# Duo attention and routed experts on one core: v loaded in 512-byte runs and ordered by TensorE, streaming heads scored in blocks of 64 queries

## The chip, the core and the metric

The kernel runs on one core of a Trainium2 chip. The metric is the device time in microseconds (us) of one execution; lower is better. Its engines run in parallel, each through its own instruction stream in order: PE (TensorE, matmuls and transposes into PSUM), DVE (VectorE), ACT (ScalarE), POOL (GpSimd) and SP (SyncE, which here only issues DMAs). They meet through semaphores. PSUM has eight banks of 2 KB a partition, and every buffer in it belongs to a pool with a fixed number of banks.

## What is computed

The reference is an attention with two kinds of heads, followed by a mixture of experts:

```python
# q, k, v: (4, 8, 768, 64); is_retrieval = [1, 0, 1, 0, 0, 0, 1, 0]; n_sink 4; window 64
causal = rel >= 0                       # rel = query position - key position
stream_keep = causal & (is_sink | (rel < window))
mask = causal for a retrieval head, stream_keep for a streaming head
a = softmax(where(mask, q @ k.T / 8, -1e9)); attn = a @ v
x = attn.transpose(0, 2, 1, 3).reshape(3072, 512)
do_compute = x @ w_skip > 0             # the other rows are handed through
e_idx = argmax(x @ w_gate); gate_w = softmax(x @ w_gate)[e_idx]
out = x + gate_w * (relu(x @ w1[e_idx]) @ w2[e_idx])   # for rows that compute
```

So a query of a retrieval head sees all earlier keys, and a query of a streaming head sees the last 64 keys and keys 0 to 3, the sinks. There are 12 retrieval and 20 streaming heads.

## The kernel before

**Pairs and steps.** The 32 heads are taken as 16 pairs of neighbouring heads (`heads`, L474). In each batch three pairs hold a retrieval and a streaming head, and one (pairs 2, 6, 10 and 15) holds two streaming heads. The loop at L852 runs 18 steps. Step i scores pair i, weighs pair i-1, transposes q and k of pair i+1 and casts those of pair i+2. Two steps behind come the transposes of the result for the gate.

**The order is written by hand.** The block at L832 puts PE, DVE, POOL and ACT under `manual_schedule`: on these four an instruction stands where the program writes it. SP isn't among them. The order in a step: `step(0)` (the first score chunk), k transposes, `step(1)`, q transposes, `weigh(i-1, 0)`, `step(2)`, `cast_qk(i+2)`, `step(3)`, `gate_transpose(i-2)`, `weigh(i-1, 1)`, `step(4)`. Every fourth step adds the choice of an expert for a batch (`choose`, L717), the step after it the places of the tokens (`gate_weight`, `place`, `left`, `right`; L754 to L828). `left` makes six compares on DVE that write Lall (L812), `right` makes oht (L818) and Rall (L822).

**q and k.** SP loads fp32 tiles (L484), POOL casts them to fp16 (L499), PE transposes them into a `tr_ps` bank, named tps (L518). ACT copies q from there (L526). DVE copies k (L535) into `kz`, one half of the partitions for each head and zeros in the other; in a pair of two streaming heads ACT copies the second half (L537).

**v.** SP loads v with the position within a block of 128 as the partition (L395, L492), in runs of 64 fp32, 256 bytes. At the start of step i POOL casts it into `va` (L505), which also holds a column of ones for the sum of the weights. For a streaming head POOL copies `va` to `vx` (L510) and overwrites its first four partitions with the sinks' values (L511).

**Scores.** A chunk is up to 1024 columns of a `st_ps` buffer, pst, of which there are two, each two banks. PE first writes a mask (L578, the identity times a mask of 0 and -30000), and adds k times q to it (L588). ACT takes the exponential into `at` (L606). A retrieval head has 2688 columns, three chunks. A streaming head has 1408, two chunks of 1024 and 384: six diagonal blocks of 128 x 128, and five blocks that hold the previous block's last 64 keys on 64 partitions (L595) and, on the other 64, the sinks (L600).

**Weighing.** `weigh` (L609) multiplies `at` with `va` or `vx`, 65 columns a matmul (L626), into one of two `ov_ps` banks, opsa: 21 matmuls for a retrieval head, 11 for a streaming head. DVE takes the reciprocal of the sums (L637, rec) and scales (L641, xh). POOL casts the scaled pair to fp16 (L649, gx) for the gate, and SP stores xh (L654, L660). Behind five of these casts POOL issues a load of expert weights (L650). PE transposes gx into a `tr_ps` bank (L667, xtp) and ACT copies it out (L675).

**The experts.** After the last batch's places, POOL gathers the chosen rows (L958), PE runs two matmuls an expert (L994, L1014), ACT applies relu (L1001), DVE adds (L1022), POOL scatters (L1024), and between them POOL loads the remaining weights.

**PSUM in the attention.** st_ps takes four banks, tr_ps two, ov_ps two. In tr_ps stand all of tps, xtp, the gate's logits gps and the counts kps, in turn.

Of the kernel before, what the change touches and what calls it, by code (L numbers as in the profile page):

```python
# [259 lines left out]
def kernel(  # L260
# [100 lines left out]
    for e in range(E // 2):  # L361
        for half in range(2):
            wtile(e, half, wpool)
    wtile(E // 2, 0, wpool)
# [30 lines left out]
    vv = v.rearrange("b h (n p) d -> b p h n d", p=P)  # L395
# [11 lines left out]
    SLEN = (2 * NQB - 1) * P  # L407
    CH = 1024

    with tc.tile_pool(name="ac", bufs=1) as ac_pool, \  # L410
# [5 lines left out]
         tc.tile_pool(name="tr_ps", bufs=2, space=bass.MemoryType.PSUM) as tr_psum, \  # L416
         tc.tile_pool(name="at", bufs=2) as at_pool, \
         tc.tile_pool(name="ov_ps", bufs=2, space=bass.MemoryType.PSUM) as ov_psum, \
# [20 lines left out]

        NPR = B * H // 2  # L440
        qk32, v32, qk16, qT, ats, xhs, x16s, xTs = ({} for _ in range(8))
        gpss = {}

        def make_masks():
# [5 lines left out]
            def select(m, base, column, row):  # L450
                nc.gpsimd.affine_select(
                    out=m, in_=m, compare_op=ALU.is_ge, fill=-MASKED,
                    base=base, pattern=[[column, P]], channel_multiplier=row)
# [4 lines left out]
            band = ac_pool.tile([P, P], FP16, name="band")  # L458
            nc.gpsimd.memset(band, 0.0)
            select(band, 0, 1, -1)  # L460
            select(band, WINDOW - 1, -1, 1)
            saux = ac_pool.tile([P, P], FP16, name="saux")
            nc.gpsimd.memset(saux, 0.0)
            select(saux, WINDOW - 1 - P, -1, 1)
            nc.gpsimd.memset(saux[:N_SINK], 0.0)
            smask = ac_pool.tile([P, 2 * NQB - 1, P], FP16, name="smask")
            nc.vector.tensor_copy(
                smask[:, :NQB], band.unsqueeze(1).to_broadcast([P, NQB, P]))
            nc.vector.tensor_copy(smask[:N_SINK, 0], rmask[:N_SINK])
            nc.vector.tensor_copy(  # L470
                smask[:, NQB:], saux.unsqueeze(1).to_broadcast([P, NQB - 1, P]))
            return smask.rearrange("p n c -> p (n c)"), rmask
# [15 lines left out]
        def load_v(i):  # L488
            b, hs = heads(i)
            vf = ld_pool.tile([P, 2, NQB, D], FP32, tag="vf", name="vf")  # L490
# [12 lines left out]
        def cast_v(i):  # L503
            va, vx = vab[i % 2], vxb[i % 2]
            nc.gpsimd.tensor_copy(va[:, :, :, :D], v32[i])  # L505
            if i % 4 == 3:
                nc.scalar.activation(xgs[(i + 1) // 4], xgs[0], ACT.Copy)
            for hi, hh in enumerate(heads(i)[1]):
# [598 lines left out]
```

## Time and profile before

| | |
|---|---|
| median of three runs | 208.47 us (208.34 to 209.57) |
| the profiled execution | 209.57 us |
| its span, first to last instruction | 208.0 us |
| busy: PE, DVE, ACT, POOL | 169.1, 113.1, 113.7, 120.0 us |
| mean granted clock of PE | 0.928 |
| first exponential (ACT L606) | 9.09 us |
| last value before the gather (DVE flagi) | 131.0 us |
| last matmul of the experts | about 198 us |
| q, k loads; v loads | 16 each of 384 KB; 32 of 192 KB |
| DMA packets under 512 bytes | 28,500 of 48,000 |

The page of a profile gives busy times, the span in 40 slices (each digit a busy share in tenths, PEclk the clock granted to PE), and groups of instructions. A line of the waits reads: engine and line that waited, who ended the wait, us in total, how often, the longest. A line of the timeline reads: start, duration, engine, line, operation, what it writes and reads, how many were merged, and in brackets the idle time before it with its releaser. A line of the windows reads: stretch, its length, busy time and number of instructions of each engine, PEclk, DMA share, GB/s. In all of them L-numbers are lines of the kernel.

### The profile page before, as it was taken

How to read it: one execution, taken by the hardware profiler on the slowest of the kernel's cores; microseconds unless marked ns; L12 is line 12 of the kernel's file. 1: busy time of each engine (PE TensorE's matmuls, PEld its weight loads, DVE VectorE, ACT ScalarE, POOL GpSimd, SP SyncE). 2: the span in 40 equal slices, each digit the busy share in tenths (PEclk: the TensorE clock that was granted, in tenths of full speed). 3: DMA queues.
4: the chain of work that ended last, by engine and by line, in shares of the span. 5: the costliest groups of instructions: out<-in, count | busy, mean ns of one | idle time of the engine just before them, and what ended most of it. 6: DMA issues, size and time to landing. Idle time of an engine off the chain costs nothing.

```text
span 208.0 us, 4783 instructions
## 1 busy us (share of the span) xinstructions
PE 169.1 (81%) x1904; PEld 121.7 (59%) x1904; DVE 113.1 (54%) x278; ACT 113.7 (55%) x164; POOL 120.0 (58%) x180
## 2 busy tenths in 40 slices
PE   6596979978991878996989737988999999999920
PEld 2365657756671656674776524367587688675700
DVE  5333756635899435899835878233555344544020
ACT  2358769995993395996699528214242243140400
POOL 7584698759565439564573502588868675133311
PEclk9969999999997599999699985699999999999995
DMA  5999599999899996899869989999999999999601
GB/s 180 293 340 294 136 178 285 318 337 313 227 237 262 292 276 172 257 268 189 241 119 215 223 189 190 196 212 217 267 242 231 230 234 238 227 250 251 169 8 61
DMA packets 48000, 47.12 MB, mean 227 GB/s; under 512 B 28500, under 2 KB 43604, under 8 KB 47074
## 3 DMA queue, kind: packets, MB, share of 16 engines
q0 software_dynamic: 7120, 21.56, 49.3%
q1 hardware_dynamic: 40850, 25.17, 43.5%
q8 instruction: 17, 0.28, 0.5%
q14 instruction: 13, 0.11, 0.2%
HBM read 56.64 MB, written 10.49 MB: 323 GB/s over the span
## 4 chain that ended last, share of the span: by engine, by line
DMA 17%; DVE 12%; issue 9%; POOL 8%; PE 6%; ACT 1%; POOLq 1%; DVEq 0%
DMA out_dram<-xg,idx_s 14%; POOL xg L958 4%; DMA xg<-out_dram,idx_s 4%; POOL out_dram L1024 3%; DVE Lall L812 3%; DVE xh L641 2%; PE opsa L626 1%; DVE kz L535 1%; PE pst L588 1%; DVE oht L818 1%; PE tps L518 1%; PE pst L578 1%; DVE Rall L822 1%; POOLq L1067 1%; DVE val L762 1%
## 5 line engine op out<-in xcount | busy, mean ns | idle before, releaser
L606 ACT ACTIVATE at<-pst 128x1024 f16<-128x1024 f32 (+2 forms) x76 | 61.9, 836 | 17.9 <-PE pst L588 10.7
L1001 ACT ACTIVATE ht<-hps 128x512 f16<-128x512 f32 x32 | 19.1, 598 | 45.4 <-PE hps L994 45.4
L588 PE MATMUL pst<-qT,kz 128*128 128x128 f16 (+2 forms) x288 | 36.3, 243 | 3.3 <-DVE kz L535 2.8
L535 DVE COPY kz<-tps 64x768 f16<-64x768 f16 x28 | 26.7, 953 | 18.6 <-PE tps L518 18.3
L588 PEld LDWEIGHTS <-kz 128*128 128x128 f16 x288 | 24.1, 101 | 17.7 <-issue 7.0
L649 POOL CAST gx<-xh 128x768 f16<-128x768 f32 x15 | 12.4, 826 | 35.5 <-DVE xh L641 30.7
L994 PE MATMUL hps<-xT,w 128*128 128x256 f16 x256 | 29.3, 273 | 1.1 <-DVE xT L984 1.1
L994 PEld LDWEIGHTS <-w 128*128 128x128 f16 x256 | 27.9, 113 | 2.7 <-issue 1.4
L1014 PE MATMUL yps<-w,ht 128*128 128x512 f16 x128 | 28.8, 379 | 0.0
L1024 POOL DMA_INDIRECT out_dram<-xg,idx_s x16 | 16.5, 1031 | 19.1 <-issue 9.1
L578 PE MATMUL pst<-smask,ident 128*128 128x512 f16 (+1 forms) x60 | 22.1, 368 | 4.3 <-ACT at L606 4.2
L1022 DVE SCALAR_TENSOR_TENSOR xg<-yps,gsl,xg 128x512 f32<-128x512 f32 x16 | 12.0, 751 | 20.5 <-PE yps L1014 20.4
L958 POOL DMA_INDIRECT xg<-out_dram,idx_s x16 | 17.1, 1071 | 9.0 <-DVE flagi L933 4.5
L1014 PEld LDWEIGHTS <-ht 128*128 128x128 f16 x128 | 12.3, 98 | 13.5
L626 PE MATMUL opsa<-va,at 128*128 128x65 f16 x372 | 20.0, 197 | 0.0
L641 DVE TENSOR_TENSOR xh<-opsa,rec 128x384 f32<-128x384 f32 x32 | 17.8, 557 | 1.3
L626 PEld LDWEIGHTS <-at 128*128 128x128 f16 x472 | 18.4, 100 | 0.2
L637 DVE RECIPROCAL rec<-opsa 128x6 f32<-128x6 f32 x32 | 6.2, 195 | 20.1 <-PE opsa L626 19.8
L526 ACT ACTIVATE qT<-tps 128x768 f16<-128x768 f16 x16 | 13.0, 814 | 5.8 <-PE tps L518 5.8
L675 ACT ACTIVATE gxT<-xtp 128x768 f16<-128x768 f16 x15 | 12.1, 809 | 6.2 <-PE xtp L667 6.2
L974 DVE CAST x<-xg 128x512 f16<-128x512 f32 x16 | 9.7, 639 | 10.5 <-DMA xg<-out_dram,idx_s 10.5
L667 PE MATMUL xtp<-ident,gx 128*128 128x128 f16 x96 | 8.5, 227 | 8.4 <-DVE kz L535 4.8
(121 smaller groups left out, 278.8 us busy)
## 6 DMA issues: line engine op xcount, KB each, us to landing
w<-in_moe_w_dram POOLq DMA_DIRECT2D x13, 1024.0 KB, 10.8
qf<-in_q_dram SPq DMA_DIRECT2D x16, 384.0 KB, 5.7
kf<-in_k_dram SPq DMA_DIRECT2D x16, 384.0 KB, 5.9
vf<-in_v_dram SPq DMA_DIRECT2D x32, 192.0 KB, 5.5
out_dram<-xh SPq DMA_DIRECT2D x7, 768.0 KB, 4.9
w<-in_moe_w_dram POOLq DMA_DIRECT2D x6, 512.0 KB, 9.0
out_dram<-xh SPq DMA_DIRECT2D x2, 384.0 KB, 5.4
xg<-out_dram,idx_s POOLq DMA_INDIRECT x16, 7.6
```

What stands on the lines that cost most here:

```text
L526: nc.scalar.activation(t16.rearrange("d (p n) -> d p n", n=NQB), ti, ACT.Copy)
L535: nc.vector.tensor_copy(to, ti[r])
L578: nc.tensor.matmul(pst[:, bank - c0:bank - c0 + mw], C.ident, rmask.unsqueeze(1).to_broadcast([P, mw // P, P]) if retr else smask[:, bank: ...
L588: nc.tensor.matmul(pst[:, cols], kz[:, j * P:(j + 1) * P], qT[i][:, qb * P:(qb + n) * P], start=mw <= 0, stop=mw <= 0 or last)
L606: nc.scalar.activation(ats[i][:, b0:b0 + cn], pst[:, :cn], ACT.Exp, scale=SCALE)
L626: nc.tensor.matmul(opsa[:, qb, :], ats[i][:, b0 + c:b0 + c + P], vb, start=(n == 0), stop=(n == len(plan) - 1))
L641: nc.vector.tensor_mul(xhs[i // 2][:, :, 2 * (i % 2) + hi, :], opsa[:, :, :D], rec.to_broadcast([P, NQB, D]))
L958: ins = nc.gpsimd.indirect_dma_start(out=xgs[t], out_offset=None, in_=out[:, :], in_offset=bass.IndirectOffsetOnAxis(ap=idx_s[:, t:t + 1], ...
L994: nc.tensor.matmul(hps[:, fi, :], wts[e, 0][:, s].rearrange("p (t c r) -> p t r c", c=P, r=WR)[:, fs // WR, fs % WR], xTs[e][:, s, :], sta ...
L1001: nc.scalar.activation(ht[:, 2 * f2:2 * f2 + 2], hps, ACT.Relu)
L1014: nc.tensor.matmul(ypss[s2], hts[e][:, fs, s2 * P:(s2 + 1) * P], wts[e, 1][:, fs, :], start=(fs == 0), stop=(fs == FS - 1))
L1024: ins = nc.gpsimd.indirect_dma_start(out=out[:, :], out_offset=bass.IndirectOffsetOnAxis(ap=idx_s[:, t:t + 1], axis=0), in_=xgs[t], in_off ...
```

## The change

**v.** The load now puts two neighbouring positions in one run of 512 bytes: partition p of a block of 256 positions holds positions 2p and 2p+1. POOL casts the tile as it stands into `vin` (`cast_v`), now for pair i+1 in step i, behind `cast_qk(i+2)`. In step i, behind the k transposes, `order_v(i)` brings the positions in order: two matmuls with 0/1 matrices (`pick`) for each half of the blocks of 128, 384 columns each, into two `tr_ps` banks. ACT copies the first half into `va`, DVE the second. Then POOL makes `vx` (`shift_v`), which holds the block of 128 positions shifted by 64, in two copies on 64 partitions. The zeroing copy of xg on ACT keeps its place at the start of a step (`zero`).

**Streaming heads.** Scores are made in blocks of 64 queries against 128 keys, which cover the window, and the sinks' scores of five blocks of 128 queries are packed in two further blocks, on 4 partitions from each of 0, 32, 64 and 96. That makes 1024 columns, one chunk. The sinks' values lie in a new tile `vsk` for all heads, zero elsewhere, zeroed by DVE and filled by four DMAs from POOL at the start. The masks are made anew for it. A streaming head is weighed by 16 matmuls.

**Pools.** tr_ps has three banks and ov_ps one; the last head's sums go to a st_ps buffer. Two tiles of expert weights (w2 of expert 3, w1 of expert 4) go from the first weight pool to the one that opens when the attention's pools are closed; the order of the loads stays.

The core of the diff (left out: the score loop's parts for streaming heads that go, and names):

```diff
-    vv = v.rearrange("b h (n p) d -> b p h n d", p=P)
+    vv = v.rearrange("b h (m p n) d -> b p h m (n d)", p=P, n=2)
...
-    SLEN = (2 * NQB - 1) * P
+    SLEN = (NQB + 2) * P
...
-         tc.tile_pool(name="tr_ps", bufs=2, space=bass.MemoryType.PSUM) as tr_psum, \
+         tc.tile_pool(name="tr_ps", bufs=3, space=bass.MemoryType.PSUM) as tr_psum, \
...
-         tc.tile_pool(name="ov_ps", bufs=2, space=bass.MemoryType.PSUM) as ov_psum, \
+         tc.tile_pool(name="ov_ps", bufs=1, space=bass.MemoryType.PSUM) as ov_psum, \
...
+        def clear_sinks():
+            for hs in (slice(1, H, 2), slice(4, 5)):
+                nc.vector.memset(vsf[:, :, hs].bitcast(FP32), 0.0)
+            for g in range(4):
+                nc.vector.memset(
+                    vsk[32 * g:32 * g + N_SINK, :, :, g, D:], 1.0)
+
+        def sink_values():
+            for g in range(4):
+                nc.gpsimd.dma_start(
+                    out=vsk[32 * g:32 * g + N_SINK, :, :, g, :D].rearrange(
+                        "p b h d -> p (b h) d"),
+                    in_=v.rearrange("b h s d -> s (b h) d")[:N_SINK])
...
         def cast_v(i):
+            v16[i] = qk_in_pool.tile([P, 2, NQB // 2, 2, D], FP16, tag="vin",
+                                     name="vin")
+            nc.gpsimd.tensor_copy(
+                v16[i].rearrange("p h m n d -> p h m (n d)"), v32[i])
+
+        def order_v(i):
+
             va, vx = vab[i % 2], vxb[i % 2]
-            nc.gpsimd.tensor_copy(va[:, :, :, :D], v32[i])
+            for half in range(2):
+                vps = tr_psum.tile([P, 2, NQB // 2, D], FP32, tag="tps",
+                                   name="vps")
+                for n in range(2):
+                    nc.tensor.matmul(vps, pick[:, half, n],
+                                     v16[i][:, :, :, n], start=n == 0,
+                                     stop=n == 1)
+                to = va[:, :, half::2, :D]
+                if half == 0:
+                    nc.scalar.activation(to, vps, ACT.Copy)
+                else:
+                    nc.vector.tensor_copy(to, vps)
+            shift_v(i)
...
+        def shift_v(i):
+            va, vx = vab[i % 2], vxb[i % 2]
             for hi, hh in enumerate(heads(i)[1]):
                 if not IS_RETR[hh]:
-                    nc.gpsimd.tensor_copy(vx[:, hi], va[:, hi, :NQB - 1])
-                    nc.gpsimd.tensor_copy(
-                        vx[:N_SINK, hi], va[:N_SINK, hi, 0:1].to_broadcast(
-                            [N_SINK, NQB - 1, D + 1]))
+                    nc.gpsimd.tensor_copy(vx[:D, hi], va[:D, hi, 1:])
+                    nc.gpsimd.tensor_copy(vx[D:, hi], va[D:, hi, :NQB - 1])
...
+        def score_near(i, hi, pst):
+
+            kz, qt = kzb[i % 2][:, hi], qT[i]
+            for bank in range(2):
+                nc.tensor.matmul(
+                    pst[:, bank * 512:(bank + 1) * 512], C.ident,
+                    smask[:, bank * 512:(bank + 1) * 512], start=True,
+                    stop=False)
+            nc.tensor.matmul(pst[:, :P], kz[:, :P], qt[:, :P], start=False,
+                             stop=False)
+            for t in range(3, 2 * NQB, 2):
+                cols = slice(t * D, (t + 1) * D)
+                nc.tensor.matmul(pst[:, cols], kz[:, (t - 1) * D:(t + 1) * D],
+                                 qt[:, cols], start=False, stop=False)
+            for t in range(2, 2 * NQB, 2):
+                cols = slice(t * D, (t + 1) * D)
+                for r, u in ((0, t), (D, t - 1)):
+                    nc.tensor.matmul(pst[r:r + D, cols],
+                                     kz[:, u * D:(u + 1) * D], qt[:, cols],
+                                     start=False, stop=t == 6)
+            for qb in (5, 1, 2, 3, 4):
+                g, c = (qb - 1) % 4, NQB + (qb - 1) // 4
+                nc.tensor.matmul(
+                    pst[32 * g:32 * g + 32, c * P:(c + 1) * P], kz[:, :32],
+                    qt[:, qb * P:(qb + 1) * P], start=False, stop=qb < NQB - 1)
...
+                vs = vsk[:, b, hs[hi]]
+                plan = [(qb, (NQB + (qb - 1) // 4) * P, vs[:, (qb - 1) % 4])
+                        for qb in range(1, NQB)]
+                plan.append((0, 0, va[:, hi, 0]))
+            near = [] if IS_RETR[hs[hi]] else [
+                (t, vx[:, hi, t // 2 - 1] if t % 2 == 0 else va[:, hi, t // 2])
+                for t in range(2, 2 * NQB)]
+            if i == NPR - 1 and hi == 1:
+                last_ps = st_psum.tile([P, CH], FP32, tag="pst", name="opsl")
...
+            for t, vb in near:
+                r = (t % 2) * D
+                nc.tensor.matmul(
+                    opsa[r:r + D, t // 2, :],
+                    ats[i][:, b0 + t * D:b0 + (t + 1) * D], vb, start=False,
+                    stop=t >= 2 * NQB - 2)
...
             lower_mask()
+            clear_sinks()
             load_qk(2)
             transpose(0, "q")
             transpose(0, "k")
+            cast_v(0)
+            load_v(2)
             cast_qk(1)
+            sink_values()
             for i in range(NPR + 2):
                 cur = chunks(i) if i < NPR else []
-                if i < NPR:
-                    cast_v(i)
                 if i + 3 < NPR:
                     load_qk(i + 3)
-                if i + 2 < NPR:
-                    load_v(i + 2)
+                if i < NPR:
+                    zero(i)
...
                 step(0)
                 if i + 1 < NPR:
                     transpose(i + 1, "k")
+                if i < NPR:
+                    order_v(i)
...
                 if i + 2 < NPR:
                     cast_qk(i + 2)
+                if i + 1 < NPR:
+                    cast_v(i + 1)
+                if i + 3 < NPR:
+                    load_v(i + 3)
...
-        for e in range(E // 2, E):
+        for e in range(E // 2 - 1, E):
```

## The prediction

> **What bounds the kernel now.** I read the page first, then the waits, then the timeline engine by engine, and last a table of windows around the stalls. In the page's slices (1 slice = 5.2 us) the experts fill slices 26 to 38 and the attention all before them:
>
> ```profile
> PE   6596979978991878996989737988999999999920
> DVE  5333756635899435899835878233555344544020
> ACT  2358769995993395996699528214242243140400
> POOL 7584698759565439564573502588868675133311
> PEclk9969999999997599999699985699999999999995
> ```
>
> From 138 us on PE is full at full clock (58.87 us busy of 60.00 in the window 138 to 198). The change touches nothing there, so the end moves by what the attention moves. In the attention no engine is the bound alone. A step with a retrieval and a streaming head (step 4, 34.52 to 39.87 us) keeps PE going without a wait for 5.35 us, and ACT needs about 5.1. Where a step takes longer, these waits say why:
>
> ```profile
> POOL gx L649 <- DVE xh L641: 30.7, 13, 5.3
> PE xtp L667 <- DVE kz L535: 4.8, 1, 4.8
> PE pst L578 <- ACT at L606: 4.7, 7, 1.2
> POOL qin L499 <- DMA qf<-in_q_dram: 2.2, 3, 1.4
> POOL kin L499 <- DMA kf<-in_k_dram: 1.3, 4, 0.4
> ```
>
> PE's longest wait is for kz on DVE, and loads cost 3.5 us in all, nearly all before 15 us. No engine waits for v. The DVE, POOL and PE timelines show the long wait:
>
> ```profile
> 54.68 1.94 DVE L535 COPY kz<-tps 64x768 f16<-64x768 f16 x2 [0.32 <-PE tps L518]
> 57.87 1.48 DVE L762 CAST val<-gate 128x6 f16<-128x6 f32 x1
> 61.03 4.19 DVE L812 TENSOR_SCALAR Lall<-iota,row 128x128 f16<-128x128 f16 x6
> 66.20 1.92 DVE L535 COPY kz<-tps 64x768 f16<-64x768 f16 x2
> ```
>
> ```profile
> 61.75 0.83 POOL L505 CAST va<-vf 128x768 f16<-128x768 f32 x1
> ...
> 63.58 0.82 POOL L499 CAST qin<-qf 128x768 f16<-128x768 f32 x1
> 64.35 0.82 POOL L499 CAST kin<-kf 128x768 f16<-128x768 f32 x1
> ```
>
> ```profile
> 68.17 0.80 PE L667 MATMUL xtp<-ident,gx 128*128 128x128 f16 x6 [4.79 <-DVE kz L535]
> ```
>
> The six Lall compares take 4.19 us while POOL casts beside them. At 127.68, with POOL idle, the same six take 1.07. The kz copies of the next pair stand behind them, PE runs dry, and its clock is 0.50 from 65.2 to 72.0 us:
>
> ```profile
> 60.00:65.20 5.20, 3.35 (x53) 2.66 (x51) 5.13 (x12) 4.40 (x6) 4.06 (x6) 1.00 1.05 209
> 65.20:72.00 6.80, 3.83 (x34) 2.89 (x34) 4.34 (x11) 1.30 (x2) 1.53 (x2) 0.50 1.11 299
> ```
>
> The same returns at 91.58 (Lall 2.87 us, oht 2.05). I use the starts of kz on DVE as milestones: pair 4 at 30.69, 8 at 54.68, 9 at 66.20, 10 at 72.44, 12 at 85.94, 14 at 100.60, 15 at 106.49; the last value for the experts' gather stands at 131.0.
>
> **The skill.** The Trainium skill, "GPSIMD Engine Reference", section Specifications, says that GpSimd shares its SBUF interfaces with VectorE, with contention when DVE is in a two-port mode or reads two SBUF inputs. The trace agrees (4.19 against 1.07 us). "VectorE: DVE Perf Modes", section on the TRN2 errata, prices a PSUM source at 120 plus its elements in cycles of 0.96 GHz: 925 ns for 768, where the trace has 953. "TensorE: Matmul & The Clock Gate", What's actually happening, gates the clock to a half after an idle window of about 3.4 us; 0.50 after the 4.79 us wait agrees. The same page, Part 3, says that matmuls on different column groups run side by side; in the trace a 384-column L600 starts at 39.59 and its successor on the other 64 outputs at 39.66.
>
> **PE.** Ordering v adds 4 matmuls of 384 columns, 1536 columns a pair. The 1024 columns of L588 at 35.63 are done in 0.44 us, so +0.65. A streaming head's scores now take 1.09 + 0.55 = 1.64 us (37.55 to 38.64, 39.32 to 39.87). After: 1024 mask columns 0.44, one of 128 0.06, fifteen of 64 at 0.03 (21 matmuls of 65 columns take 0.66) 0.45, five of 128 0.28: 1.23, or 1.0 if the halves overlap fully. I take 1.1: -0.54. Weighing goes from 11 to 16 matmuls: +0.16. A mixed step: +0.27, to 5.62 us; the step with two streaming heads (5.4 now): about 5.3.
>
> **ACT.** A streaming head drops its 384-wide exp (20 heads, 0.39 us each counting overlap, -7.8). Half of v in 16 pairs has the same size (+6.2). Net -1.6 over the whole attention, nothing on one step's pace.
>
> **DVE.** The other half of v, 384 fp32 from PSUM, isn't in the trace. L678 (384, fp16 source) took 0.36, L641 (two inputs) 0.56, the skill's row gives an estimate of 0.525. I take 0.50, and keep 0.36 to 0.56.
>
> **POOL.** cast_v costs what it did (0.83). A streaming head's two vx copies were 0.457 (128 partitions) and 0.449 (4 partitions) and become two on 64 partitions: width hardly matters, so the same. What changes is the order. Before, va, vx, q and k ran in one go behind gx, on top of DVE's gating work. Now shift_v waits for DVE's half of v, which stands behind kz, and behind shift_v stand the casts of the pair after next. That is a new loop from k to k:
>
> - PE transposes and latency 0.53 (35.30 to 35.83)
> - kz on DVE 1.93, half of v 0.50, handover 0.1
> - shift_v 0.93 (1.84 with two streaming heads), from starts at 26.66, 27.18, 27.58
> - q and k casts 1.59, handover 0.1
>
> It makes 5.68 us, or 6.6 with two streaming heads. PE needs 5.62, so I take 5.8 and 6.6. Where the next kz's second half is on ACT (0.83 more there), ACT sets 6.2.
>
> **Buffers.** tps has three banks, and most q transposes reuse the bank that ACT's half of v frees, before exp 1 is through: cover 0.92 us of exp, no stall. One opsa bank makes weigh(i-1,1) wait for rec and xh of weigh(i-1,0), 0.95 us: hidden behind two score chunks in mixed steps, partly open (about 0.5) with two streaming heads, inside the 6.6. SP's v loads come three pairs ahead but wait for cast_v; q and k loads behind them have two steps of some 6 us for a 5.7 us landing. The w2_3 and w1_4 tiles move to the later pool; POOL loads them behind the gathers in both kernels, when attention is over: nothing.
>
> **The sum by milestones.**
>
> - *To kz of pair 4* (30.69): DVE gets new work before the first kz: zeroing 2080 and 520 fp32 a partition (512 take 0.485, so 2.0 to 2.2 and 0.5), picks and masks about 1.7. DVE was idle 2.6 there, so first kz goes from 7.32 to about 9.1. Four sink DMAs cost POOL about 0.75 each, hidden while it waits for DVE. Step 1 is regained, since POOL was late anyway, but in step 2 shift_v waits for v, behind DVE's routing constants (22.57 to 24.9), and the k casts of pair 4 behind it end near 31.7 (now 30.09): +1.5. If the start is covered, 0.
> - *4 to 8* (23.99 now): 5.8 + 5.8 + 6.2 + 6.6 = 24.4: +0.4.
> - *8 to 10* (17.76 now). On DVE from kz 8: 1.93 + 0.5 + 0.76 + gate_weight 2.1 (POOL still casts beside it) + 0.7 + 0.76. Then the Lall group meets only gx: 0.16 + 1.4 + 1.0 instead of 5.4. That is 9.3 to kz 9; then 1.93 + 0.5 + 0.1 + 0.93 + 1.59 + 0.1 + 0.53 to kz 10. 15.0: -2.7. PE's dry spell falls to about 2 us, so I expect the full clock.
> - *10 to 12* (13.50 now): 6.2 + 6.7 = 12.9: -0.6.
> - *12 to 14* (14.66 now): 15.0: +0.35. Here PE had run further ahead, so the shorter Lall buys little.
> - *14 to 15* (5.89): 6.0, +0.1.
> - *15 to the end of attention* (24.5): weigh(14,0) stands behind two full streaming chunks and v: +0.65; a bank that DVE frees holds the gate's logits: +0.3; compares beside fewer POOL copies: -0.4. +0.55.
>
> Total +1.5 +0.4 -2.7 -0.6 +0.35 +0.1 +0.55 = -0.4. Span 208.0 to 207.6; the profiled execution itself took 209.57, 1.57 around its span, but the median of the runs is 208.47. On that median: 208.1, which I round to 208.0.
>
> **The rivals.**
>
> - *The stalls go altogether.* Cast L762 isn't held either (-0.9 each time), Lall falls to 1.07 (-0.3), turns run at PE's 5.5 (about -2 in nine turns), the start is half hidden (-0.8): 208.0 less 2.4, 2 and 0.8, some 203, and I put 204. For it: the 11.5 us from kz 8 to 9 is the largest hole. Against: PE and ACT need over 5 us a step.
> - *The loop through POOL sets every turn.* If a vx copy on 64 partitions takes a third more (0.62), a mixed turn grows by 0.32 and one with two streaming heads by 0.64: six and four of these, 1.9 + 2.6, gives 212.5. It decides once the loop exceeds PE's 5.62 clearly, at 6 us. For it: the order behind the new waits. Against: 4 partitions cost as much as 128.
> - *The transfers matter.* A packet of v (256 B) took 18 ns in the median of the trace's packets, a 512 B store 27. 24,576 x 20 / 16 = 31 us of all engines' time becomes 12,288 x 27 / 16 = 21. Hidden, as no one waits for v; at the start it could bring pair 1 forward by 0.5, and under the 3.5 us of load waits at most 2: 206. If nothing comes of it, that is the forecast.
>
> **Chances.** The forecast with its own range 206 to 210.5: 0.42. The first rival 0.26, the loop 0.24, the transfers 0.08. A measurement tells about 1% from no change, 206.4 to 210.6. Faster: 0.26 and half of 0.08 and 0.04 of the forecast, 0.34. Slower: 0.24 and 0.04, 0.28. Within: 0.38. The range 203.5 to 212.5 covers both rivals' values.
>
> **What would show it.** The Lall row near 1.4 us and kz 8 to 9 near 9.3; k casts starting right behind vx and PE waiting for them in steps after two streaming heads; first kz near 9.1; clock 1.00 from 30 to 100 us; load waits unchanged. It is wrong if 64-column matmuls cost like 128-column ones (15 x 0.025 = 0.4 us a head), if POOL's copies slow, or if PE's waits at the start grow past 2 us.

## The result, and the profile after

The changed kernel took 218.23 us in the median (217.93 to 218.63), the kernel before 209.02 beside it: a ratio of 1.0441, 95% interval 1.0393 to 1.049. It is slower by 4.4%, outside the range of the prediction. The profiled execution has a span of 216.8 us against 208.0. Some executions of a kernel are slower than its others by one or two per cent; the medians count them, the ratios leave them out.

The page's slices (5.4 us each now) answer to those of before:

```profile
PE   6378986999899599897798965898899999999930
DVE  6773475643699745799545596724343445244120
POOL 6746866677556463763765512188785864224311
PEclk9959999999999979999799965579999999999995
```

The experts again fill the end and take what they took; the last value before them (flagi) comes at 139.97 us instead of 131.23. All 8.7 us are lost in the attention. By the milestones, the starts of kz on DVE (from one pair's kz to the next is a turn; in a mixed turn the pairs at work have one retrieval and one streaming head each):

| stage | before | predicted | after |
|---|---|---|---|
| to kz of pair 4 | 30.69 | +1.5 | 34.52, +3.8 |
| 4 to 8 | 23.99 | +0.4 | 27.11, +3.1 |
| 8 to 10 | 17.76 | -2.7 | 14.98, -2.8 |
| 10 to 12 | 13.50 | -0.6 | 15.22, +1.7 |
| 12 to 14 | 14.66 | +0.35 | 14.97, +0.3 |
| 14 to 15 | 5.89 | +0.1 | 7.03, +1.1 |
| 15 to flagi (131.23 before) | 24.74 | +0.55 | 26.14, +1.4 |

The waits of the changed kernel, whole execution, show who stands now:

```profile
POOL vx L573 <- DVE rec L724: 16.2, 7, 4.5
DVE kz L596 <- PE tps L579: 12.3, 10, 3.4
POOL vx L573 <- DVE va L562: 10.6, 4, 3.3
POOL gx L736 <- DVE xh L728: 7.1, 7, 2.7
PE opsa L707 <- DVE xh L728: 5.8, 6, 1.8
POOL vx L573 <- ACT va L560: 5.1, 4, 1.7
```

Before, POOL waited at gx, behind its casts (30.7 us in all). Now it waits at vx, ahead of them: 16.2, 10.6 and 5.1 us. (Where rec is named, DVE's copy of va ends just as rec begins, and vx reads va.) The chain of waits through two turns, from the view of what ended last (start, us, what), shows how a turn is made up:

```profile
36.50 0.56 DVE va L562
...
37.19 0.46 POOL vx L573
...
37.70 0.46 POOL vx L574
...
38.22 0.82 POOL qin L538
39.05 0.77 POOL kin L538
39.81 0.78 POOL vin L545
...
40.64 0.81 PE vps L555 x4
...
46.48 0.96 DVE kz L596
...
48.30 0.49 ACT va L560
48.79 0.92 ACT at L654
...
49.76 0.59 PE pst L661 x2
...
54.22 0.50 ACT va L560
...
54.76 0.74 PE gps L792 x24
...
57.09 0.68 PE opsa L707 x21
...
58.02 0.56 DVE xh L728
...
59.24 0.74 DVE eq L818
...
61.63 0.94 DVE kz L596
```

The first part is a mixed turn: v on DVE, vx, the three casts, and PE, which takes up vps only once v of the next pair is cast (40.59). The second part runs from kz of pair 6 to kz of pair 8. ACT's half of v stands ahead of an exp, PE stands behind that exp, the gate's logits stand behind ACT's next half of v, the weighing behind them, and kz behind `choose` on DVE. These two turns (from pair 6, with two streaming heads, to pair 8) took 7.18 and 7.97 us.

What the change was to bring at 8 to 10 is there: on DVE's timeline the six compares take 1.64 us instead of 4.19.

```profile
67.81 1.64 DVE L899 TENSOR_SCALAR Lall<-iota,row 128x128 f16<-128x128 f16 x6
```

### The profile page after: what moved, and what is told of

It reads as the page before. It is cut to its first block, busy times and chain, and to the rows that moved or that the text cites. A ratio compares the mean times of both kernels' runs of the same rounds, so it can differ in the third digit from the quotient of the medians.

```text
span 216.8 us, 5474 instructions
## 1 busy us (share of the span) xinstructions
PE 180.1 (83%) x2208; PEld 128.6 (59%) x2208; DVE 120.8 (56%) x312; ACT 113.6 (52%) x160; POOL 121.9 (56%) x184
## 3 DMA queue, kind: packets, MB, share of 16 engines
q1 hardware_dynamic: 28562, 25.17, 36.7%
## 4 chain that ended last, share of the span: by engine, by line
DVE 27%; PE 24%; DMA 18%; POOL 13%; issue 12%; ACT 2%; POOLq 1%; DVEq 0%; ACTq 0%
DMA out_dram<-xg,idx_s 18%; DVE kz L596 6%; POOL xg L1053 5%; PE pst L648 4%; PE tps L579 4%; PE opsa L707 3%; DVE xh L728 3%; PE pst L661 3%; DVE Lall L899 3%; PE vps L555 3%; DVE va L562 2%; POOL out_dram L1119 2%; PE pst L674 2%; POOL qin L538 2%; POOL kin L538 1%
## 5 line engine op out<-in xcount | busy, mean ns | idle before, releaser
L654 ACT ACTIVATE at<-pst 128x1024 f16<-128x1024 f32 (+1 forms) x36 | 33.1, 919 | 15.2 <-PE pst L648 14.7
L573 POOL COPY vx<-va 64x325 f16<-64x325 f16 x20 | 9.0, 452 | 34.3 <-DVE rec L724 16.2
L648 PE MATMUL pst<-qT,kz 128*128 128x128 f16 (+2 forms) x168 | 23.3, 263 | 4.9 <-DVE kz L596 4.9
L633 ACT ACTIVATE at<-pst 128x1024 f16<-128x1024 f32 x20 | 20.5, 1023 | 9.8 <-PE pst L679 8.9
L648 PEld LDWEIGHTS <-kz 128*128 128x128 f16 x168 | 14.5, 104 | 10.4 <-DVE kz L596 5.4
L707 PEld LDWEIGHTS <-at 128*128 128x128 f16 x372 | 14.7, 99 | 8.7 <-DVE xh L728 6.8
L728 DVE TENSOR_TENSOR xh<-opsa,rec 128x384 f32<-128x384 f32 x31 | 17.3, 557 | 1.0
L555 PE MATMUL vps<-vin,pick 128*128 128x384 f16 x64 | 14.9, 361 | 1.9 <-POOL vin L545 0.7
L538 POOL CAST qin<-qf 128x768 f16<-128x768 f32 x16 | 13.2, 824 | 1.6 <-DMA qf<-in_q_dram 0.7
```

The source lines that it names most:

```text
L538: nc.gpsimd.tensor_copy(h16, qk32[name, i].rearrange("p h n d -> p n h d"))
L555: nc.tensor.matmul(vps, pick[:, half, n], v16[i][:, :, :, n], start=n == 0, stop=n == 1)
L633: nc.scalar.activation(ats[i][:, b0:b0 + SLEN], pst, ACT.Exp, scale=SCALE)
L648: nc.tensor.matmul(pst[:, c - c0:c - c0 + n * P], kzb[i % 2][:, hi, j * P:(j + 1) * P], qT[i][:, qb * P:(qb + n) * P], start=mw <= 0, stop ...
L654: nc.scalar.activation(ats[i][:, b0:b0 + cn], pst[:, :cn], ACT.Exp, scale=SCALE)
L707: nc.tensor.matmul(opsa[:, qb, :], ats[i][:, b0 + c:b0 + c + P], vb, start=(n == 0), stop=(n == len(plan) - 1 and not near))
```

## The experiments

In the table, ratios are to the kernel before on the same chip, with the 95% interval; the stages are from one profiled execution each. "End" is flagi. Differences between kernels in us are taken from the ratios below (1% is 2.09 us) unless they are of stages. Kernels whose orders differ only later lie up to 1.0 us apart at kz of pair 4 (31.92 and 30.89 in e6 and e9, 34.52 and 33.83 in the changed kernel and e14), so a difference of stages below 1 us shows little. For e4 no stages are given.

| kernel | median us | ratio | first kz | kz 4 | 4-8 | 8-12 | 12-15 | end |
|---|---|---|---|---|---|---|---|---|
| before | 209.0 to 209.5 | 1 | 7.32 | 30.69 | 23.99 | 31.26 | 20.55 | 131.23 |
| after | 218.23 | 1.0441 (1.0393-1.0490) | 11.08 | 34.52 | 27.11 | 30.20 | 22.00 | 139.97 |
| e1_pools | 211.18 | 1.0080 (1.0049-1.0112) | 7.17 | 30.20 | 22.99 | 30.28 | 24.10 | 132.81 |
| e2_order | 222.09 | 1.0539 (1.0471-1.0607) | 6.74 | 32.98 | 28.08 | 32.85 | 23.20 | 144.23 |
| e3_near | 208.35 | 0.9942 (0.9907-0.9976) | 9.32 | 31.80 | 25.71 | 27.60 | 20.02 | 130.32 |
| e4_after22 | 231.11 | 1.0997 (1.0940-1.1055) | | | | | | |
| e5_shift | 219.03 | 1.0477 (1.0408-1.0547) | 10.38 | 32.20 | 27.00 | 31.15 | 24.53 | 140.97 |
| e6_late | 215.99 | 1.0345 (1.0272-1.0418) | 10.99 | 31.92 | 24.63 | 30.49 | 24.10 | 137.04 |
| e7_runs | 3834.19 | see below | 9.32 | 31.96 | 23.10 | 28.45 | 19.41 | 128.09 |
| e8_start | 218.36 | 1.0461 (1.0392-1.0530) | 8.14 | 36.44 | 27.10 | 29.81 | 21.27 | 140.75 |
| e9_late_lr | 210.56 | 1.0046 (1.0021-1.0072) | 10.40 | 30.89 | 25.01 | 27.71 | 19.47 | 130.12 |
| e10_before_lr | 205.67 | 0.9760 (0.9696-0.9825) | 6.86 | 31.04 | 24.00 | 26.89 | 18.42 | 127.21 |
| e11_near_lr | 208.38 | 0.9904 (0.9871-0.9937) | 9.93 | 31.43 | 25.68 | 26.00 | 18.59 | 128.35 |
| e12_near_lr_act | 208.00 | 0.9895 (0.9831-0.9958) | 7.12 | 31.24 | 25.17 | 26.02 | 18.61 | 128.11 |
| e13_order_only | 232.79 | 1.1082 (1.1031-1.1133) | 10.39 | 37.24 | 32.50 | 35.36 | 23.18 | 154.19 |
| e14_after_lr | 217.03 | 1.0369 (1.0321-1.0418) | 10.38 | 33.83 | 27.10 | 29.90 | 20.81 | 138.78 |
| e15_act_late | 225.94 | 1.0766 (1.0724-1.0808) | 11.01 | 35.88 | 31.36 | 33.14 | 22.16 | 148.85 |
| e16_near_lr_v3 | 209.19 | 0.9982 (0.9951-1.0013) | 9.33 | 33.57 | 24.58 | 25.99 | 18.60 | 128.81 |
| e17_shift_lr | 210.44 | 1.0063 (1.0036-1.0090) | 10.37 | 32.12 | 26.03 | 27.52 | 18.95 | 131.67 |
| e18_v_best | 210.76 | 1.0082 (1.0048-1.0116) | 7.09 | 30.66 | 25.32 | 27.35 | 19.73 | 130.97 |

### Which part costs: e1 to e4

My first theory was that the single opsa bank and the start on DVE cost the time; the rival, that the loop over POOL does. e1 and e2 build the change up from the kernel before, e3 makes the streaming part alone, e4 takes back the banks.

e1, in the kernel before:

```diff
-         tc.tile_pool(name="tr_ps", bufs=2, space=bass.MemoryType.PSUM) as tr_psum, \
+         tc.tile_pool(name="tr_ps", bufs=3, space=bass.MemoryType.PSUM) as tr_psum, \
-         tc.tile_pool(name="ov_ps", bufs=2, space=bass.MemoryType.PSUM) as ov_psum, \
+         tc.tile_pool(name="ov_ps", bufs=1, space=bass.MemoryType.PSUM) as ov_psum, \
```

> The kernel before with one edit: tr_ps three banks, ov_ps one. Theory (one opsa bank makes the second head's weighing wait for rec and xh of the first): the waits on the opsa line rise from 0 to some 4 us in all, a part of it open, and the time is 1 to 3 us above the kernel before. Rival (the bank is hidden, as the prediction had it, and a third tps bank gives back what it costs): within 0.5 us of the kernel before.

Measured: +0.8%, at the low end of the theory. PE waited 12.8 us at opsa for xh, in three waits, instead of some 4. Yet the turns from 4 to 12 did not get longer (4 to 8: 22.99 against 23.99); what grew is 12 to 15, by 3.6 us.

e2 is e1 with the diff's v part (the new `vv`, `pick`, `cast_v` a step ahead, `order_v`) and the old `vx`:

```diff
+                if i < NPR:
+                    order_v(i)
...
+                if i + 1 < NPR:
+                    cast_v(i + 1)
```

> e1 and, on top, the v part alone: 512-byte runs, the cast a step ahead, ordering by PE, the copies by ACT and DVE, vx made behind it with its old two copies; streaming heads are scored as in the kernel before (the two weight tiles move as in the change). Theory (the loop from kz over DVE's half of v, vx and the casts to the next kz sets the turns): 3 to 5 us above e1, and the time to kz of pair 4 only about 1 us later, since no sinks are cleared. Rival (the order of v is harmless, the streaming part is what costs): within 1 us of e1.

Measured: 1.0539, 9.6 us above e1. The loss is the v part's, and about twice the most that either theory allowed. Against e1 it comes in every stage but the first kz (6.74) and 12 to 15, and 1.9 us of it behind kz of pair 15 (27.1 us to flagi against 25.2).

e3 is the changed kernel with `load_v`, `cast_v` and the pools of before:

```diff
-                    order_v(i)
+                    cast_v(i)
...
+            nc.gpsimd.tensor_copy(va[:, :, :, :D], v32[i])
```

> The streaming part alone: blocks of 64 queries with packed sinks, sinks cleared at the start, v loaded and cast as in the kernel before, two tr_ps and two ov_ps banks. Theory (what this part costs is the start on DVE): first kz 1.5 to 2.5 us later than before, that delay kept to the end, and the turns no longer than before, so 1 to 3 us above the kernel before. Rival (64-column matmuls or the single 1024-column chunk make each turn longer): 4 us or more above, with turns longer by 0.3 us each. Rival (ACT's saving pays): at or below the kernel before.

Measured: 0.9942. The streaming part alone gains about 1 us, though its first kz is 2 us late; the compares take 2.65 and 2.87 us. So neither the 64-column matmuls nor the single chunk are the loss. Where the gain comes from shows only in e11.

e4 reverses e1's edit in the changed kernel.

> The changed kernel with the banks as before: tr_ps two, ov_ps two. Theory (the single opsa bank costs more than the third tps bank brings): 2 to 4 us below the changed kernel, the waits of the opsa line on xh gone. Rival (the third tps bank is what lets v be ordered beside the transposes): 1 us or more above the changed kernel, with waits of the v and q transposes on the copies of ACT and DVE.

Measured: 1.0997, 11.6 us above the changed kernel. My theory falls, and the rival holds: two banks for v, both transposes, xtp and the logits are too few. In its trace v's matmuls wait 8.5 us for ACT's copies of v and 4.7 us for ACT's copies of kz. Beside v's order the third bank is worth far more than the second opsa bank.

### The order on POOL, and the compares: e5, e14, e17

e5 moves one call in the changed kernel:

```diff
-            shift_v(i)
...
                 if i + 1 < NPR:
                     cast_v(i + 1)
+                if i < NPR:
+                    shift_v(i)
```

> The changed kernel with one call moved: shift_v (vx on POOL) stands behind the casts of q, k and v of the step instead of ahead of them, so that those casts no longer wait for DVE's half of v. Theory (what v costs is PE's and ACT's place in the step: ordering and its copies stand ahead of the second chunk and its exp): within 1.5 us of the changed kernel. Rival (the loop from kz over v, vx and the casts to the next kz sets the turns, the prediction's second rival): 3 to 6 us below the changed kernel.

Measured: no gain. That looked like the end of the loop over POOL, but its profile says otherwise: kz of pair 4 comes 2.3 us earlier, and the compares are held up again. DVE's and POOL's timelines of e5:

```profile
65.15 3.53 DVE L898 TENSOR_SCALAR Lall<-iota,row 128x128 f16<-128x128 f16 x6
```

```profile
65.94 0.82 POOL L538 CAST qin<-qf 128x768 f16<-128x768 f32 x1
66.71 0.82 POOL L538 CAST kin<-kf 128x768 f16<-128x768 f32 x1
67.48 0.82 POOL L545 CAST vin<-vf 128x768 f16<-128x768 f32 x1
```

Once vx no longer holds the casts back, they run behind gx and beside the compares (3.53 and 4.26 us), as in the kernel before. So I moved the compares, which needs `posi` only:

```diff
                     gate_weight(b)
                     place(b)
+                    left(b)
+                    right(b)
...
-                if late == 1:
-                    left(b)
-                    right(b)
```

> The changed kernel with left and right moved up, directly behind place, and nothing else. Theory (in the changed kernel POOL already waits while the compares run, 1.64 us, so the move frees nothing): within 1.5 us of the changed kernel. Rival (the move is worth what it was in e9 and e10, whatever the order of v): 3.5 to 5.5 us below it.

> The changed kernel with vx behind the casts (e5) and left and right moved up, order_v where the change has it. Theory (the loss is the sum of three orders, and the compares gave back in e5 what vx behind the casts had freed): 4 to 6 us below e5, so 213 to 215 us, and what stays to e9 (2 to 4 us) is the place of order_v. Rival (the place of order_v decides alone): within 1.5 us of the changed kernel.

The four corners, as ratios to the kernel before:

| | vx ahead of the casts | vx behind them |
|---|---|---|
| compares where they were | 1.0441 (change) | 1.0477 (e5) |
| compares directly behind `place` | 1.0369 (e14) | 1.0063 (e17) |

Each move alone brings 0.7% at most, both bring 3.8 of the 4.4%. That is not the share that these orders have in the loss, for the move of the compares also helps the kernel before (e10 below, 0.976). Beside e10, with the compares in the same place, e14 is 6.2% slower and e17 3.1%: vx ahead of the casts accounts for about half of what the change costs there, and the other half stays in e17. With vx ahead of the casts, POOL stops behind gx until v of the next turn is ready: the compares meet gx alone, and the casts are late in every turn. With vx behind, the casts follow gx at once and fall on the compares. In e17, which did better than its theory (213 to 215 us), all compares take 1.07 us, and `choose` is free of casts too: on DVE's timeline, the changed kernel

```profile
59.24 0.73 DVE L818 SCALAR_TENSOR_TENSOR eq<-sub,erev 128x48 f32<-128x48 f32 x1
60.24 0.46 DVE L824 SCALAR_TENSOR_TENSOR m<-glog,m 128x6 f32<-128x6 f32 x1
```

and e17:

```profile
56.57 0.21 DVE L817 SCALAR_TENSOR_TENSOR eq<-sub,erev 128x48 f32<-128x48 f32 x1
57.05 0.17 DVE L823 SCALAR_TENSOR_TENSOR m<-glog,m 128x6 f32<-128x6 f32 x1
```

That is 0.8 us of the 7.97 us turn.

### The place of order_v: e6, e9, e13, e15

e6 is e5 with

```diff
                 step(2)
+                if i < NPR:
+                    order_v(i)
                 if i + 2 < NPR:
                     cast_qk(i + 2)
```

and without the call behind the k transposes.

> e5 and, on top, order_v behind the third chunk instead of behind the k transposes. Theory (ordering ahead of the second chunk delays exp, the first weighing and, in steps with the choice of experts, DVE's chain): 3 to 6 us below e5, with 4 to 8 shorter by 1.5 us. Rival (PE's added 0.65 us a pair is what costs, wherever it stands): within 1 us of e5. Rival (the bank that holds v is then missing for xtp): slower than e5.

Measured: 2.8 us below e5, just under what was expected and with overlapping intervals; 4 to 8 is 2.4 us shorter. The compares still take 3.53 and 4.26 us. e9 is e6 with e14's edit.

> e6 (order_v behind the third chunk, shift_v behind the casts) with left and right moved up, directly behind place, ahead of the second head's weighing. In e6 the six compares of Lall took 3.5 and 4.3 us again. Theory (what is left of the loss after e6 is mainly those compares beside POOL's casts): compares at 2 us or less, 8 to 10 and 12 to 14 each 1.5 to 2.5 us shorter, the time 3 to 5 us below e6. Rival (xh then stands 3 us later and PE waits for the one opsa bank instead): within 1 us of e6.

Measured: 6.2 us below e6, a little more than expected. But e17, with order_v where the change has it, is as fast as e9 (1.0063 and 1.0046). e9's turns 4 to 8 are 1.0 us shorter, its 8 to 10 is 1.4 longer (14.61 against 13.21). The expectation that 2 to 4 us hang on this place falls.

e13 is e6's edit without e5's: vx stays ahead of the casts, and comes later, since v does.

> The changed kernel with order_v behind the third chunk, and shift_v still ahead of the casts (half of e6). Theory (two orders hold each other: ordering delays PE and ACT, and vx on POOL delays the casts, so only both moves together help): no gain or a loss, since vx, and the casts behind it, now come later: 0 to 4 us above the changed kernel. Rival (the place of order_v alone is what costs): 2 to 3 us below the changed kernel, as far as e6.

Measured: 1.1082, 13.4 us above the changed kernel, far more than the 0 to 4 I gave. PE's waits from 30 to 128 us, then POOL's and DVE's timelines of e13:

```profile
PE tps L579 <- POOL kin L538: 17.3, 10, 3.7
```

```profile
41.79 0.45 POOL L573 COPY vx<-va 64x325 f16<-64x325 f16 x1 [3.61 <-DVE va L562]
...
43.60 0.82 POOL L538 CAST kin<-kf 128x768 f16<-128x768 f32 x1
```

```profile
37.24 1.94 DVE L596 COPY kz<-tps 64x768 f16<-64x768 f16 x2 [3.27 <-PE tps L579]
...
41.10 0.56 DVE L562 CAST va<-vps 128x384 f16<-128x384 f32 x1 [1.10 <-PE vps L555]
...
45.02 1.93 DVE L596 COPY kz<-tps 64x768 f16<-64x768 f16 x2 [1.16 <-PE tps L579]
```

From the end of va (41.66) to the next kz are 3.36 us: vx, two casts, the transposes. The turn is 7.78 us because va ends 4.42 us behind kz, where in the changed kernel it ends 2.54 behind (34.52 to 37.06). That is the loop over POOL. It hands the delay of va on nearly one to one: va ends 1.88 us later behind kz than in the changed kernel, and the turn is 1.75 us longer.

e15 delays only ACT's half of v, and vx with it:

```diff
                 step(1)
+                if i < NPR:
+                    nc.scalar.activation(*first_half[i], ACT.Copy)
                 if i + 1 < NPR:
                     transpose(i + 1, "q")
...
+                if i < NPR:
+                    shift_v(i)
                 step(2)
```

> The changed kernel with only ACT's half of v copied later, behind the exp of the second chunk, and vx made behind it, still ahead of the casts. PE and DVE order as in the change. Theory (ACT's copy ahead of the second exp is a large part of what the place of order_v costs): 1 to 2.5 us below the changed kernel, turns from pair 6 on shorter. Rival (PE's four matmuls ahead of the second chunk, or vx on POOL, cost it): within 1 us of the changed kernel.

Measured: 6.8 us above the changed kernel, the other way than expected. I had looked at ACT's queue alone; vx moved with the copy, and the casts with vx. In the mixed turns this is e13's loop again (6.65 and 6.71 us for 6.03 and 5.93). Most of the loss lies elsewhere: the two turns with `choose` take 11.2 and 10.8 us instead of 7.97. In the first of them the chain doesn't pass through POOL's casts but through the logits, xh and `choose` on DVE, which those casts, now later, run beside.

### The start: e8 and e12

e8 builds `pick` and clears the sinks behind `transpose(0, "k")`:

```diff
-            clear_sinks()
...
             transpose(0, "k")
+            make_pick()
+            clear_sinks()
```

> The changed kernel with DVE's new work of the start (pick, clearing of the sinks) behind the first pair's kz instead of ahead of it. Theory (that work is what delays the start): first kz near 8 us instead of 11.1, kz of pair 4 about 2 us earlier and the time 1.5 to 3 us below the changed kernel. Rival (the same work then stands ahead of pair 1's kz, or the POOL order of the first steps takes the gain): kz of pair 4 within 0.7 us of the changed kernel's.

e12 is e11 with the sinks cleared by ACT.

> e11 with the sinks cleared by ACT, which has little to do there, instead of DVE. Theory (DVE's clearing ahead of the first kz is what delays the start): first kz near 7 us instead of 9.3, and 1 to 2 us below e11. Rival (loads and POOL's casts set the first steps, so an earlier first kz is lost by kz of pair 4): within 0.5 us of e11.

Measured: first kz comes 2.9 and 2.8 us earlier, and nothing is left of it. In e8 the work only moves ahead of pair 1's kz (15.34 instead of 14.01), so it doesn't show what the work costs. In e12 ACT takes it over, and kz of pair 4 is where it was in e11. In e9 kz of pair 4 is at 30.89 with a first kz at 10.40. So in these two orders a late first kz is made up by pair 4; no run takes the work away in the changed kernel's own order.

### Transfers: e7, e11, e16

e7 is e3 with v in 512-byte runs:

```diff
-            nc.gpsimd.tensor_copy(va[:, :, :, :D], v32[i])
+            nc.gpsimd.tensor_copy(
+                va[:, :, :, :D], v32[i].rearrange(
+                    "p h m (n d) -> p h (m n) d", n=2))
```

> The streaming part alone (e3) with v loaded in 512-byte runs and the ordering left out: POOL casts the runs straight into va, so that rows of v stand in another order than the keys. It shows what the runs themselves bring. Theory (v loads are hidden): within 0.7 us of e3. Rival (the transfers matter): 1 to 2 us below e3, with the load waits shorter.

With v out of order the program took another branch after the attention, so only its attention is compared: it ended at 128.09 us, e3's at 130.32. All of that is in one turn, from pair 5 to 6 (7.54 us in e3, 5.16 here), where POOL in e3 waited for a load:

```profile
40.10 0.83 POOL L534 CAST va<-vf 128x768 f16<-128x768 f32 x1 [2.88 <-DMA vf<-in_v_dram]
```

e11 is e3 with the compares moved up; e16 is e11 with `bufs=3` for vf and `load_v(i + 3)`.

> The streaming part alone (e3) with left and right moved up. Theory: compares near 1.1 to 1.6 us instead of 2.65 and 2.87, 1.5 to 3 us below e3, so 2 to 4 us below the kernel before. Rival (e3's own gain at 8 to 10 was this same gain): within 0.7 us of e3.

> e11 (streaming part alone, left and right moved up) with a third buffer for v's loads, issued three pairs ahead. In e3 and e11 POOL waits 2.9 us for a load of v near 37 us, and the next kz comes 7.5 us after the last instead of 5.2. Theory (v in 256-byte runs comes late there, which takes the streaming part's gain): the wait goes, and the time is 1.5 to 3 us below e11. Rival (more loads in flight only move the wait to q and k): within 0.7 us of e11.

e11 gained 0.4%, intervals overlapping, less than expected: 1.6 us at 8 to 10 and 0.8 at 12 to 14 came, but the late load is still there (7.74 us from pair 5 to 6). So its rival is close: e3's gain at 8 to 10 (14.61 us for 17.76) was largely this same gain. Beside e10 (below), which is the kernel before with the same move, e11 is 1.4% slower. With the compares out of the way the streaming part is thus a loss of 3 us, and 1.7 of these stand at 4 to 8, where the late load is. e16 took away the wait of POOL's cast for v and put 6.5 us of waits for q in its place; it is slower than e11 (0.9982, intervals apart). The rival holds: more loads in flight moved the wait and did not shorten it.

### A version that beats both: e10; and v at its best: e18

e10 is the kernel before with e14's edit alone.

> The kernel before with left and right moved up, directly behind place. Theory (the hole from kz of pair 8 to kz of pair 9 comes of the compares that run beside POOL's casts, which gx releases): compares near 1.1 to 1.6 us, 8 to 10 shorter by about 2.5 us, 12 to 14 by 1 to 2, the time 3 to 5 us below the kernel before. Rival (the later xh takes it back): within 1 us of the kernel before.

Measured: 205.67 us, 0.976 (0.9696 to 0.9825), as expected, and the fastest of all; the interval leaves open whether it gains more than 2%. On DVE's timeline:

```profile
60.75 1.07 DVE L812 TENSOR_SCALAR Lall<-iota,row 128x128 f16<-128x128 f16 x6
...
63.50 1.91 DVE L535 COPY kz<-tps 64x768 f16<-64x768 f16 x2
```

kz of pair 9 comes 8.46 us behind kz of pair 8 (11.52 before). In the turns the later xh costs nothing that shows. At the end something does: kz of pair 15 comes 6.1 us earlier than before, flagi 4.0. In all five kernels that differ from another by this move alone (e9, e10, e11, e14, e17) the stretch from pair 15 to flagi is 1.0 to 2.1 us longer; what in the move costs this isn't shown. With the compares gone, the loads begin to show: POOL's cast of v waits 5.5 us for them, not at all before.

e18 is e2 with e5's, e6's and e14's edits.

> The v part alone (e2: streaming heads as before, three tr_ps banks and one ov_ps bank) in the order of e9: order_v behind the third chunk, vx behind the casts, left and right moved up. Beside e10 it shows what ordering v costs where its order is good. Theory (then only PE's 0.65 us a pair and the one opsa bank are left): 3 to 7 us above e10, so 209 to 213. Rival (ordering v costs PE's and ACT's time in any order): as far above e10 as e2 above e1, some 11 us.

Measured: 210.76 us, 1.0082, 6.7 us above e10. The theory holds, at its upper end: two thirds of what the v part cost in the change's order (9.6) remain in this one. What the 512-byte runs bring in exchange isn't shown in this order; e7 put it at about 2 us beside e3.

## Why the prediction was wrong, point by point

- *The gain at 8 to 10* was right in size (-2.8 for -2.7) and mechanism: POOL waits, Lall takes 1.64 us (about 1.4 expected), kz 8 to 9 is 8.80 (9.3). There is luck in the -2.8: kz 9 to 10 took 6.18 us instead of 5.68, and the two errors cancel. 12 to 14 was right too. But the gain needed no part of the change (e10), and in the changed kernel it is paid for by the wait that brings it. The full clock that was to come with it did not: PE's longest wait there was 1.81 us, as forecast, and the clock still was 0.50 from 76 to 78 us. Nor does the kernel before agree with the idle window that the prediction cites for its clock: at 65.5 us PE had been idle for only 2.1 us, and the clock was at 0.50 already. What sets it isn't shown.
- *The step that failed: "It makes 5.68 us, or 6.6 with two streaming heads. PE needs 5.62, so I take 5.8 and 6.6 ... ACT sets 6.2."* The loop was right, and mixed turns came near (6.03 and 5.93). The turns around two streaming heads took 7.18 and 7.97 for 6.2 and 6.6, and again 7.25 and 7.97 in 10 to 12: together 4.7 us of the 9.1 by which the sum missed. I took the longest single loop for the turn. The chain shows one path over several engines: kz and v on ACT, exp, then PE without a gap from 49.76 to 53.2 over two full chunks; then the logits behind ACT's v, the weighing, xh and `choose` on DVE ahead of kz. POOL was done with k at 59.9, and kz came at 61.63. The runs confirm two pieces of this path: with `choose` free of casts (e17) the turns from pair 6 to 8 take 0.8 us less, and with v ordered later (e9) another 1.2 us less, 13.1 us in place of 15.2. The forecast was 12.8; the rest isn't divided.
- *To kz of pair 4, +1.5*: measured +3.8. I had named the start on DVE and vx behind late v. e9 and e12 make up a late first kz by pair 4, so the start need not cost anything; e5 and e17, with vx behind the casts, win 2.3 and 2.4 us. So vx cost more than I gave for both. The other 1.4 us have no run that names their cause; they are small only where v is ordered later as well (e6 and e9, 31.92 and 30.89).
- *14 to 15 and the end* missed by 1.0 and 0.9 us. e17 wins 1.1 in the first. At the end e1 and e3, where POOL writes v, take 25.2 us from pair 15 to flagi, and e2, which orders it by PE, 27.1: the v part costs there. Which of its pieces does isn't settled.
- *"One opsa bank ... hidden"*: in the kernel before it costs 0.8% (e1), but not in the turns, and e9 and e17 run near the time of before with one bank. That v stalls nothing with the third tps bank was right, and too little said: without it 11.6 us more (e4).
- *The second rival* named the right loop, over POOL, for the wrong reason. A vx copy on 64 partitions took 0.45 us, as before, not 0.62; the copies waited. The mixed turns took 6.03 and 5.93 us, at the 6 us that it gave as the point from which the loop decides.
- *The transfers*: v's loads land in 4.4 us instead of 5.5, and nobody waited for them in the kernel before. Where the loads are late, they bring about 2 us (e7, one execution). The change had no such wait left to win.
- *ACT* was to be busy 1.6 us less and is not (113.6 us for 113.7). The streaming part brought what it was to bring (e3 106.3), but half of v took 0.49 us a pair, not 0.39.

What stays open: where the 6 to 7 us lie by which e17 and e18 stand above e10. In e18 PE is busy 8.8 us longer (176.1 against 167.3) and waits 7.8 us for xh at the one opsa bank, and the stages are longer by 0.5 to 1.3 us in five places.

## What to carry to other kernels

In an engine's queue, put no copy that waits for a product of this turn ahead of the work that feeds the next turn: price a moved instruction by who stands behind it, and test it by delaying it (e13, e15), not only by freeing it. When a wait seems to bring a gain, ask what the work does once it is freed, and move that work's victim too: e5 and e14 alone show next to nothing, and together 3.8%. Then make the second move in the kernel before as well: without e10, all of these 3.8% would have been put down to the change. Around a step of another kind, follow one chain over all engines instead of taking the longest engine.

## What was not expected of the hardware

While the four loads of the sinks' values (16 KB each, POOL's queue) run, other loads hardly move. e3 shows it, as SP goes on issuing loads there: v at 14.08 us, q at 15.98, k at 16.75. From 15 to 20 us, 40 columns of 0.125 us, the transfers of e3:

```profile
GB/s 74 76 72 53 61 43 45 22 15 17 21 10 31 10 4 2 2 6 10 12 27 14 12 39 25 29 41 80 49 55 27 23 14 29 27 37 25 18 31 41
...
q1 hardware_dynamic: 469, 0.12, 126.1%
q0 software_dynamic: 950, 0.03, 59.6%
...
qf<-in_q_dram SPq DMA_DIRECT2D x1, 384.0 KB, 8.8
kf<-in_k_dram SPq DMA_DIRECT2D x1, 384.0 KB, 9.5
```

and of the kernel before:

```profile
GB/s 258 234 233 231 221 221 240 279 256 213 207 277 322 332 340 344 356 369 393 356 369 356 381 369 363 342 314 303 297 285 285 266 248 236 223 227 223 236 232 260
...
q1 hardware_dynamic: 3011, 1.44, 121.8%
...
qf<-in_q_dram SPq DMA_DIRECT2D x1, 384.0 KB, 6.2
kf<-in_k_dram SPq DMA_DIRECT2D x1, 384.0 KB, 6.3
```

In e3, 950 packets of POOL's queue (q0) move 0.03 MB, some 30 bytes each on average. SP's loads (q1) move 0.12 MB in these 5 us instead of 1.44, and the q and k loads issued there land 8.8 and 9.5 us after their issue instead of 6.2 and 6.3. The mean is 31 GB/s, against 287 before. In the changed kernel it is 27, but that hole shows less: SP, waiting for POOL's cast of q, issues no load from 10.2 to 18.5 us there. No run was made without the sinks' loads, so that they are the cause isn't shown, nor how much of e3's late load of v some 20 us later they cost.

The contention on SBUF, which the Trainium skill ("GPSIMD Engine Reference", Specifications) names, has a size here that depends on what runs beside: the same six compares took 1.07 us with POOL idle, 1.64 beside gx alone, and 2.7 to 4.3 us where casts and copies followed gx at once (2.65 in e3, 4.26 in e5 and e6).
